# Two decode layers on one core: a new transfer and clock model in the kernel's own planner, and value loads of at most two quarters

## The chip, the cores and the metric

The kernel runs on one core of a Trainium2 chip. The metric is the device time of one execution in microseconds (us); lower is better. The engines are named as the profile names them: PE is TensorE (PEld its weight loads), DVE is VectorE, ACT is ScalarE, POOL is GpSimd and SP is SyncE, which here does nothing but issue DMAs.

## What is computed

Two identical layers follow each other for a batch of 8 sequences with one new token each. A layer is attention over a cache of 4096 positions (16 query heads on 8 cached heads, head size 256) and a small mixer with an MLP.

```python
def _A_ref(x, k_cache, v_cache, wq, wo):
    B, Sq, D = x.shape                      # 8, 1, 448
    Hq, Dh = 16, 256
    Hkv = k_cache.shape[1]                  # 8
    rep = Hq // Hkv
    q = (lambda x, *d: x.transpose(*d))((x @ wq).reshape(B, Sq, Hq, Dh), 0, 2, 1, 3)
    k = jnp.repeat(k_cache, rep, axis=1)    # cache: (8, 8, 4096, 256)
    v = jnp.repeat(v_cache, rep, axis=1)
    scores = jnp.einsum("bhqd,bhkd->bhqk", q, k) * (Dh ** -0.5)
    p = _softmax(scores, axis=-1)
    o = jnp.einsum("bhqk,bhkd->bhqd", p, v)
    return (lambda x, *d: x.transpose(*d))(o, 0, 2, 1, 3).reshape(B, Sq, Hq * Dh) @ wo
...
x = A_x
x = x + _A_ref(_layernorm(x, axis=-1), A_k_cache, A_v_cache, A_wq, A_wo)
x = x + _B_ref(_layernorm(x, axis=-1), B_w1, B_w2, B_w3, B_w4)
x = x + _A_ref(_layernorm(x, axis=-1), A_k_cache, A_v_cache, A_wq, A_wo)
x = x + _B_ref(_layernorm(x, axis=-1), B_w1, B_w2, B_w3, B_w4)
```

`_B_ref` shifts parts of its hidden vector along a sequence of length 1, which leaves zeros, so what is left of it is a layer norm and the MLP with `w3` and `w4`. Both layers read the same two caches of 134 MB each. All arrays are bfloat16.

## The kernel before, in words

**Tiles.** One cached head of one sequence, K or V, is 2 MB. It is split into four quarters ("units") of 512 KB: 128 partitions with 4 KB each. SBUF holds 30 slots of one quarter (`QUARTERS`). A DMA fetches up to four neighbouring quarters of one head at once into neighbouring slots: 512, 1024, 1536 or 2048 KB.

**What is kept.** Sequence by sequence the first layer runs over heads 0 to 7, and the second layer follows for the same sequence. Of the five "kept" heads 3 to 7, K stays in its slots from the first layer to the second (heads 3 to 6 wholly, head 7 in part), and of V seven quarters stay: all of head 7 and three of head 6 (`KEEP_K`, `KEEP_V`). Heads 0 to 2 are the "free heads": nothing of them is kept, and both layers load them. When the kept heads of a sequence are all in place, some 24 of the 30 slots are taken, and six go round.

**Work on one head.** `front()` transposes the fresh K quarters on PE (L1319, 128x128 blocks into PSUM, copied back by DVE L1250 or ACT L1251), makes the scores (L1043), and takes the softmax on DVE, POOL and ACT. `back()` multiplies with V (`pv`, L1149: eight 256-column matmuls for a quarter), adds up (`osum`, L1173), and multiplies with four rows of `wo` (`wor`, L1198). A K quarter that isn't kept gives its slot back after its score matmuls, a V quarter after its `pv`.

**Between the layers.** `mid()` runs a chain of small dependent steps for one sequence: the output of the attention is turned (L984, L987), the MLP's first product takes 56 matmuls (L838), gelu follows, its second product takes 70 (L984, L987), then come the second layer's queries (L822) and the scores on the kept K. Around this chain stand, as work that does not depend on it, the `back()` parts of the *next* sequence's three free heads, with 12 V quarters. They pass through the six slots that go round.

**The planner.** The order of the instructions is not that of the source. Every piece of work is an `Op` with an engine, a cost and dependencies. `Plan.schedule()` goes through them with a clock of its own, always takes the engine that is free first, and there the ready op with the best priority. The result is one fixed order for each engine, with semaphores. SP is in order: loads are issued in the order of their `prio`. For the next load, `next_kv()` picks how many quarters go into it (up to `most`), the slots, and so the PE instruction that it has to wait for. `late` (L203) is the time up to which it holds a load back for a longer run of free slots: `LEAD` before the planned end of the transfers in progress.

**Costs in the plan.** A load of n quarters takes `((n << 15) / 26.88e3 + 8 * 0.008) / FASTER` us (L628), that is 4.705 us for four. The transfers stand in one line with one end, `dma_end`. For PE, the planner counts "columns" in windows of 3.413 us (`WIN`). Below `COLS` of them it plans the next window with PE at the slow one of two costs. Where PE would wait and the columns of the last window are under `TARGET`, it puts in fillers: matmuls of 256 or 512 columns without use (L1522). A matmul of the chain counts `width` columns (20 to 24), a `pv` op 512, a `wor` op 448. PE's instructions are fetched in blocks of 128 pairs (`BLOCK`), at least 6 us apart (`FETCH`).

**MOST.** `back()` sets `most`, the largest load of V: `MOST` for free heads in the first layer (from the second sequence on), `MOST2` for one kept head in the second layer, 4 otherwise.

Of the kernel before, what the change touches and what calls it, by code (L numbers as in the profile page):

```python
# [32 lines left out]
BOOST = None  # L33
HOTK = 7
L2 = (3, 4, 2, 1, 0)
MOST = 4
MOST2 = 4
BACKS = (0, 1, 3)
MIX = "KKKKKFFF"
# [1 line left out]
PV0 = 0  # L41
PV1 = 0
QW, HW, YW = 24, 24, 12
SC = 448
YC = 0
Q1 = 176
# [30 lines left out]
class Plan:  # L77
# [5 lines left out]
    HOT = 3500  # L83


    ISSUE, LEAD = 4.0, 5.0
    BLOCK, FETCH = 128, 6.0
    LAT = {"pe": 0.25, "dve": 0.06, "act": 0.06, "pool": 0.05, "sp": 0.4}

    def __init__(self):  # L90
        self.ops = []
# [41 lines left out]
    def fetched(self, t, d, n, pairs, next_block):  # L133

        per = d / n
        while n:
            room = self.BLOCK - pairs % self.BLOCK
            if room == self.BLOCK:
                t = max(t, next_block)
                next_block = t + self.FETCH  # L140
            k = min(n, room)
            pairs += k
            n -= k
            t += k * per
        return t, pairs, next_block

    def schedule(self):
# [18 lines left out]
        for o in self.ops:  # L166
            if not left[o]:
                release(o, 0.0)
        dma_end = 0.0
        win, cols, warm = 0, 0, False  # L170
        recent, hot = [], False
        bank_ev = {}
# [5 lines left out]
        n = 0  # L178
# [14 lines left out]
        def next_kv(i):  # L193

            u = sp_next[i].unit
            m = 1
            while m < u.most and i + m < len(sp_next) and sp_next[i + m].unit is not None and \
                    sp_next[i + m].unit.tile is u.tile and sp_next[i + m].unit.u == u.u + m and \  # L200
                    sp_next[i + m].unit.keep == u.keep:
                m += 1
            late = max(free["sp"], dma_end - self.LEAD)  # L203
            times = sorted(set(x for x in self.free_at if x < 1e9))
            if not times:
                return None
            for t in [max(free["sp"], times[0])] + [x for x in times if free["sp"] < x <= late]:
                fit = [(k, a) for k, a in runs(t) if k >= m]
                if fit:
                    break  # L210
            else:
                t = max(late, times[0])
                m = min(m, max(k for k, a in runs(t)))
                fit = [(k, a) for k, a in runs(t) if k >= m]

            before = sp_next[i - 1].unit if i else None
            if before is not None and before.tile is u.tile:
                for k, a in fit:
                    if a <= before.slot + 1 <= a + k - m:
                        return t, m, before.slot + 1  # L220
            k = min(k for k, a in fit)
            fit = [a for k2, a in fit if k2 == k]
            q = min(fit) if u.keep else max(fit) + k - m
            return t, m, q

        while n < len(self.ops):
# [103 lines left out]
            order[e].append(o)  # L330
            n += 1
            if e == "sp":
                free[e] = t + 0.45
                start = max(t + self.ISSUE, dma_end)
                dma_end = start + o.dur
                end = dma_end
            else:
                d = o.dur
                if e == "pe":

                    w = int(t / self.WIN)
                    while win < w:
                        warm = cols >= self.COLS
                        cols = 0
                        win += 1
                    cols += d[2]
                    recent.append((t, d[2]))
                    end, pairs, next_block = self.fetched(t, d[0] if warm else d[1], d[3],
                                                          pairs, next_block)
                    d = end - t  # L350
                elif isinstance(d, dict):
                    d = d[e]
                end = free[e] = t + d
# [109 lines left out]
def bass_interleave_layers__gqa_block_cached__mixer_s_mlp__decode_kernel(  # L463
# [137 lines left out]
        return bass.AP(tensor=ap.tensor, offset=ap.offset, ap=[list(x) for x in ap.ap[:-1]] + [[0, P]])  # L601


    FASTER = 1.05

    def dma(name, dst, src, nbytes, sem, val, wr, at, row=8192):

        us = nbytes / 16 / 26.88e3 + nbytes / row / 16 * 0.008
        plan.op("sp", lambda eng: eng.dma_start(dst, src), us / FASTER, name, wr=wr, prio=at,
                dma=(sem, val))  # L610

    def dma_once(name, parts, keys, at, also=()):
# [7 lines left out]
    def issue_kv(o, n, q):  # L620

        (cache, b, h), u = o.unit.tile, o.unit.u
        src = cache[b, h].rearrange("(m s) d -> m (s d)", m=P)[:, u * 2048:(u + n) * 2048]
        dst = kv[:, q * 2048:(q + n) * 2048]
        slot_n[q] += 1
        o.emit = lambda eng: eng.dma_start(dst, src)
        o.dma = (slot_sem[q], 16 * slot_n[q])
        o.dur = ((n << 15) / 26.88e3 + 8 * 0.008) / FASTER  # L628

    plan.issue_kv = issue_kv  # L630

# [61 lines left out]
    def pe(fn, n, rd=(), wr=(), banks=(), name="chain", prio=None, width=20):  # L693

        if prio is None:
            prio = urge[0] + len(plan.ops)
        d = 0.06 + 0.026 * n
        return plan.op("pe", fn, (d, max(d, 0.06 + n * width / 1200), width * n, n), name, rd=rd, wr=wr, banks=banks, prio=prio)

    def mark(o):  # L700

# [424 lines left out]
    def back(layer, b, h):  # L1126
# [15 lines left out]
        for u in range(4):  # L1142

            def pv(t, u=u, q=vs[u]):
                last = None
                for s in range(8):
                    i = 8 * u + s
                    g4 = 32 * (i % 4)
                    last = t.matmul(ps[g4:g4 + 2, PV0:PV0 + DH], pT[nr][:, i, :],  # L1149
                                    slot_ap(q, s * 256, 256), start=(i < 4), stop=(i >= 28),  # L1150
                                    skip_group_check=True, tile_position=(0, g4))
                return last
            o = plan.op("pe", pv, (0.25, 0.46, 512, 8), "pv",
                    rd=[("pT", nr, 0), ("pT", nr, 1), ("s", vs[u], 0), ("s", vs[u], 1),
                        "pz"],
                    wr=[("pv", par, x) for x in range(u, 4)], banks=[bk])
            if u == 0:
                o.tbank = bk
            if u not in keep_v:
                o.frees = vs[u]  # L1160
# [31 lines left out]
        if k < HKV:  # L1192
            def wo_row(t):
                last = None
                for i in range(4):
                    a = (4 * h + i) * D
                    r = 64 * layer + 32 * (i % 2)
                    last = t.matmul(psR[r:r + 1, 0:D], oT[no][:, i % 2, i // 2:i // 2 + 1],  # L1198
                                    wo_sb[:, a:a + D], start=(k == 1 and i < 2),
                                    stop=(k == HKV - 1 and i >= 2),  # L1200
                                    skip_group_check=True, tile_position=(0, r))
                return last
            o = plan.op("pe", wo_row, (0.41, 0.78, 448, 4), "wor", rd=[("oT", no), "wo0"], wr=[kr],
                        banks=["R"], prio=hi)
            if k == HOTK and layer == 0:
                o.hot = True
# [375 lines left out]
```

## Time and profile before

| | us |
|---|---|
| median of 3 runs | 1109.96 |
| the three runs | 1104.91, 1109.96, 1110.28 |
| the profiled execution, its own time | 1105.82 |
| its span, first to last instruction | 1104.0 |
| mean granted clock of PE | 0.929 |

The span is what the profile's views divide up; 1.8 us of the profiled execution lie around it. "Idle before" in a group's line is the engine's idle time just before these instructions, with what ended it. "DMA share" is the mean busy share of the 16 DMA engines. A window's line gives, for a stretch of the span, each engine's busy time with the number of its instructions, then the granted clock of PE (1 is full), the DMA share and the rate in GB/s.

### The profile page before, as it was taken

To read this page: it belongs to the slowest core of one execution; us is meant where nothing else is said; L and a number is where in the kernel's file an instruction comes from. 1 tells how busy PE (TensorE), PEld (TensorE's weight loads), DVE (VectorE), ACT (ScalarE), POOL (GpSimd) and SP (SyncE) were. 2 spreads that over 40 slices of the span, in tenths; PEclk is the share of its full clock that TensorE was granted. 3 is DMA by queue.
4 is the path that set the end of the run, shared out by engine and by line. 5 is a ranking of instruction groups with operands and counts; after the bars stand their busy time and mean duration, and the time that the engine had idled before them with its cause. 6 is when DMAs were issued, how large, how long until landed. Compare 5 with 4: busy or idle time off the path is not lost.

```text
span 1104.0 us, 42700 instructions
## 1 busy us (share of the span) xinstructions
PE 964.3 (87%) x19509; PEld 772.5 (70%) x19509; DVE 577.7 (52%) x1829; ACT 294.5 (27%) x867; POOL 97.9 (9%) x275
## 2 busy tenths in 40 slices
PE   4888889898899888998889988899879998799997
PEld 4678557785578756787668865688557986597683
DVE  4245445654455544665446554555535755365554
ACT  1133112331124302343123411234123430243130
POOL 0000000000100101010010100001010010111010
PEclk9889899998999979999799998999989997999797
DMA  9999999999999999999999999999999999999993
GB/s 331 407 425 421 392 376 423 424 416 387 384 422 422 421 364 416 424 425 413 373 425 424 422 364 388 425 424 416 378 417 423 424 365 383 410 420 399 321 385 152
DMA packets 59871, 436.94 MB, mean 396 GB/s; under 512 B 6430, under 2 KB 9644, under 8 KB 36396
## 3 DMA queue, kind: packets, MB, share of 16 engines
q1 hardware_dynamic: 59684, 434.22, 97.0%
q8 instruction: 153, 2.51, 0.9%
q14 instruction: 26, 0.21, 0.0%
q10 hardware_dynamic: 8, 0.00, 0.0%
HBM read 434.18 MB, written 0.01 MB: 393 GB/s over the span
## 4 chain that ended last, share of the span: by engine, by line
PE 55%; DMA 35%; issue 4%; DVE 4%; ACT 1%; SPq 1%; POOL 0%; DVEq 0%
PE psT L1319 20%; DMA kv<-in_A_k_cache_dram 17%; PE psM L1043 14%; DMA kv<-in_A_v_cache_dram 14%; PE psP L1149 9%; DMA wo_sb<-in_A_wo_dram 4%; PE psR L1198 3%; PE psM L822 2%; PE psM L984 1%; DVE oS L1165 1%; PE psM L987 1%; DVE oS L1163 1%; PE psP L1173 1%; PE psP L1522 1%; PE psM L838 1%
## 5 line engine op out<-in xcount | busy, mean ns | idle before, releaser
L1319 PE MATMUL psT<-ident_f,kv 128*128 128x128 f32 x2752 | 381.2, 283 | 13.9 <-DMA kv<-in_A_k_cache_dram 13.8
L1250 DVE COPY kv<-psT 128x512 f32<-128x512 f32 x403 | 276.2, 690 | 155.4 <-PE psT L1319 151.7
L1319 PEld LDWEIGHTS psT<-ident_f,kv 128*128 128x128 f32 x2752 | 304.0, 144 | 38.2 <-issue 18.9
L1251 ACT COPY kv<-psT 128x512 f32<-128x512 f32 x317 | 184.8, 587 | 465.8 <-PE psT L1319 375.8
L1149 PE MATMUL psP<-kv,pT 128*2 128x256 bf16 x4096 | 185.6, 291 | 37.5 <-DMA kv<-in_A_v_cache_dram 20.1
L1043 PEld LDWEIGHTS psM<-q2T,kv 128*128 128x128 bf16 x3968 | 121.5, 99 | 50.0 <-issue 41.0
L1043 PE MATMUL psM<-q2T,kv 128*128 128x48 bf16 x3968 | 137.2, 186 | 19.9 <-issue 19.0
L1043 PEld LDWEIGHTS psM<-q1b,kv 128*128 128x128 bf16 x4032 | 131.6, 97 | 18.2 <-issue 8.6
L1043 PE MATMUL psM<-q1b,kv 128*128 128x48 bf16 x4032 | 140.4, 184 | 4.4 <-ACT pT L1116 2.6
L1149 PEld LDWEIGHTS psP<-kv,pT 128*2 128x2 bf16 x4096 | 80.6, 84 | 78.4 <-issue 30.7
L1106 POOL PARTITION_ALL_REDUCE gm<-pm x128 | 45.6, 356 | 761.0 <-DVE pm L1104 693.9
L1116 ACT ACTIVATE pT<-sS,nb,fac 128x32 bf16<-128x32 f32 x128 | 52.7, 417 | 145.4 <-DVE nb L1110 145.4
L1099 DVE COPY sS<-psM 128x64 f32<-128x64 f32 x128 | 28.6, 224 | 109.8 <-PE psM L1043 107.2
L1163 DVE CAST oS<-psP 128x256 bf16<-128x256 f32 x128 | 54.0, 422 | 57.6 <-PE psP L1149 55.8
L1198 PE MATMUL psR<-wo_sb,oT 128*1 128x448 bf16 x448 | 68.3, 390 | 5.5 <-DMA wo_sb<-in_A_wo_dram 3.2
L1120 POOL PARTITION_ALL_REDUCE Db<-rs x128 | 51.1, 400 | 209.3 <-ACT pT L1116 209.3
L1116 ACT ACTIVATE pT<-sS,nb 128x32 bf16<-128x32 f32 x128 | 40.9, 326 | 70.1 <-DVE nb L1110 70.1
L1173 PE MATMUL psP<-sel,oS 128*128 128x2 bf16 x512 | 32.1, 166 | 29.2 <-DVE oS L1165 26.7
L1173 PEld LDWEIGHTS psP<-sel,oS 128*128 128x128 bf16 x512 | 25.4, 100 | 45.1 <-DVE oS L1165 41.8
L1165 DVE TENSOR_TENSOR oS<-psP,oS 128x256 bf16<-128x256 f32 x128 | 54.2, 423 | 3.4
L822 PEld LDWEIGHTS psM<-x2c,wq_sb 128*128 128x128 bf16 x768 | 30.8, 98 | 17.1 <-issue 5.7
L1179 DVE TENSOR_TENSOR oT<-psP,rc 128x4 bf16<-128x4 f32 x128 | 20.2, 157 | 40.3 <-PE psP L1173 34.2
(172 smaller groups left out, 657.8 us busy)
## 6 DMA issues: line engine op xcount, KB each, us to landing
kv<-in_A_k_cache_dram SPq DMA_DIRECT2D x64, 2048.0 KB, 18.7
kv<-in_A_v_cache_dram SPq DMA_DIRECT2D x49, 2048.0 KB, 15.1
kv<-in_A_v_cache_dram SPq DMA_DIRECT2D x161, 512.0 KB, 7.9
kv<-in_A_v_cache_dram SPq DMA_DIRECT2D x36, 1024.0 KB, 10.2
kv<-in_A_k_cache_dram SPq DMA_DIRECT2D x44, 512.0 KB, 8.0
kv<-in_A_k_cache_dram SPq DMA_DIRECT2D x10, 1536.0 KB, 17.0
kv<-in_A_v_cache_dram SPq DMA_DIRECT2D x9, 1536.0 KB, 17.6
kv<-in_A_k_cache_dram SPq DMA_DIRECT2D x11, 1024.0 KB, 13.5
```

What stands on the lines that cost most here:

```text
L822: last = t.matmul(bank[:, at + i * step:at + i * step + copies], w, r, start=(kc == 0), stop=(kc == 3))
L1043: last = t.matmul(ps[:, SB + 2 * i:SB + 2 * i + 2 * REP], a()[:, c:256:2], bcast(rhs(c), REP, 1), start=(c == 0), stop=(c == 1))
L1116: return a.activation(pT[nr][:, :, :].rearrange("p i j -> p j i")[:, jj, :], sview[:, jj, :], ACT.Exp, bias=nb[nm][:, jj:jj + 1], scale=sc ...
L1120: plan.op("pool", lambda gp: gp.partition_all_reduce(Db[nr][:, :], rs[nr][:, :], P, RO.add), 0.5, "sum", rd=[("rs", nr, 0), ("rs", nr, 1)] ...
L1149: last = t.matmul(ps[g4:g4 + 2, PV0:PV0 + DH], pT[nr][:, i, :], slot_ap(q, s * 256, 256), start=(i < 4), stop=(i >= 28), skip_group_check= ...
L1163: plan.op("dve", lambda v: v.tensor_copy(oS[:, 0, :], po), 0.36, "o", rd=[("pv", par, x) for x in range(4)], wr=["oS0"], banks=[bk], prio=hi)
L1165: plan.op("dve", lambda v: v.tensor_tensor(oS[:, 1, :], po, oS[:, 0, :], ALU.subtract), 0.36, "o", rd=["oS0"] + [("pv", par, x) for x in r ...
L1173: last = t.matmul(ps[:, PV1 + 2 * c:PV1 + 2 * c + 2], oS[:, w, c:DH:2], sel[:, :], start=(w == 0), stop=(w == 1))
L1198: last = t.matmul(psR[r:r + 1, 0:D], oT[no][:, i % 2, i // 2:i // 2 + 1], wo_sb[:, a:a + D], start=(k == 1 and i < 2), stop=(k == HKV - 1 ...
L1250: return e.tensor_copy(dst, psT[bank][:, :])
L1251: return e.copy(dst, psT[bank][:, :])
L1319: last = t.transpose(psT[bank][:, s * P:(s + 1) * P], src, ident_f[:, :])
```

## The change

`Plan` gets 16 rings, one for each DMA engine, in place of one line of transfers: a load adds its cost to each ring, with `WAKE` more where the ring had run dry, and lands `LAND` after the last of them. A block of PE's instructions that is fetched adds `FETCH_DMA` to one ring, in turn one of the eight even ones. `ISSUE` goes from 4.0 to 1.0, `LEAD` from 5.0 to 4.0 and is measured from the mean of the rings, the latency of a DMA's signal from 0.4 to 0.05, SP's time for an issue from 0.45 to 0.4. `FASTER` goes, and a load of n quarters costs `(n << 15) / 27.2e3 + 8 * 0.009`, 4.891 us for four. In the count of columns, a matmul of the chain has 16 (`CW`) in place of its width, a `pv` op 568 in place of 512, a `wor` op 756 in place of 448. `MOST` goes from 4 to 2. `KEEP_V` stays at 7. No arithmetic on the tensors is changed.

```diff
-MOST = 4
+MOST = 2
 MOST2 = 4
...
+CW = 16
...
-    ISSUE, LEAD = 4.0, 5.0
+    ISSUE, LAND, LEAD = 1.0, 0.46, 4.0
+    RING, CARRY, WAKE = 16, (0, 2, 4, 6, 8, 10, 12, 14), 0.75
+    FETCH_DMA = 1.55
     BLOCK, FETCH = 128, 6.0
-    LAT = {"pe": 0.25, "dve": 0.06, "act": 0.06, "pool": 0.05, "sp": 0.4}
+    LAT = {"pe": 0.25, "dve": 0.06, "act": 0.06, "pool": 0.05, "sp": 0.05}
...
             if room == self.BLOCK:
                 t = max(t, next_block)
                 next_block = t + self.FETCH
+                c = self.CARRY[self.fetches % len(self.CARRY)]
+                self.fetches += 1
+                self.ring[c] = max(self.ring[c], t + self.ISSUE) + self.FETCH_DMA
...
-        dma_end = 0.0
+        self.ring, self.fetches = [0.0] * self.RING, 0
...
-            late = max(free["sp"], dma_end - self.LEAD)
+            late = max(free["sp"], sum(self.ring) / self.RING - self.LEAD)
...
             if e == "sp":
-                free[e] = t + 0.45
-                start = max(t + self.ISSUE, dma_end)
-                dma_end = start + o.dur
-                end = dma_end
+                free[e] = t + 0.4
+                for i in range(self.RING):
+                    wake = self.WAKE if t + self.ISSUE > self.ring[i] + 0.02 else 0.0
+                    self.ring[i] = max(t + self.ISSUE, self.ring[i]) + wake + o.dur
+                end = max(self.ring) + self.LAND
...
-    FASTER = 1.05
...
-        plan.op("sp", lambda eng: eng.dma_start(dst, src), us / FASTER, name, wr=wr, prio=at,
+        plan.op("sp", lambda eng: eng.dma_start(dst, src), us, name, wr=wr, prio=at,
                 dma=(sem, val))
...
-        o.dur = ((n << 15) / 26.88e3 + 8 * 0.008) / FASTER
+        o.dur = (n << 15) / 27.2e3 + 8 * 0.009
...
-        return plan.op("pe", fn, (d, max(d, 0.06 + n * width / 1200), width * n, n), name, rd=rd, wr=wr, banks=banks, prio=prio)
+        return plan.op("pe", fn, (d, max(d, 0.06 + n * width / 1200), CW * n, n), name, rd=rd, wr=wr, banks=banks, prio=prio)
...
-            o = plan.op("pe", pv, (0.25, 0.46, 512, 8), "pv",
+            o = plan.op("pe", pv, (0.25, 0.46, 568, 8), "pv",
...
-            o = plan.op("pe", wo_row, (0.41, 0.78, 448, 4), "wor", rd=[("oT", no), "wo0"], wr=[kr],
+            o = plan.op("pe", wo_row, (0.41, 0.78, 756, 4), "wor", rd=[("oT", no), "wo0"], wr=[kr],
```

Since the planner writes the order of all engines, these edits move instructions everywhere. The two built programs differ as follows:

| | before | after |
|---|---|---|
| PE matmuls | 19509 | 19624 |
| fillers of 256 columns (L1522) | 170 | 279 |
| fillers of 512 columns (L1522) | 61 | 67 |
| K and V loads of 512 / 1024 / 1536 / 2048 KB | 205 / 47 / 19 / 113 | 208 / 45 / 18 / 114 |
| quarters loaded in all | 808 | 808 |
| copies of transposed K on DVE / ACT | 411 / 317 | 427 / 301 |

## The prediction

> **What bounds the kernel now.** I read the page first: span, engines, and the rows of rate.
>
> ```profile
> span 1104.0 us, 42700 instructions
> PE 964.3 (87%) x19509; PEld 772.5 (70%) x19509; DVE 577.7 (52%) x1829; ACT 294.5 (27%) x867; POOL 97.9 (9%) x275
> ...
> DMA  9999999999999999999999999999999999999993
> GB/s 331 407 425 421 392 376 423 424 416 387 384 422 422 421 364 416 424 425 413 373 425 424 422 364 388 425 424 416 378 417 423 424 365 383 410 420 399 321 385 152
> DMA packets 59871, 436.94 MB, mean 396 GB/s; under 512 B 6430, under 2 KB 9644, under 8 KB 36396
> ```
>
> The transfers never rest and do at best about 425 GB/s. 436.94 MB at 424 GB/s are 1030.5 us, so 73.5 us of the span are lost: at both ends, and in dips that come once a sequence, some 130 us apart, in which the rate falls to 364 to 388. The change moves the same 808 quarters, so only these 73.5 us can move. Next, windows: one in mid-stream, then the dip at 530 us and the one at 655 (the eight dips are called by their times: 135, 268, 398, 530, 655, 790, 925, 1030).
>
> ```profile
> 600.00:620.00 20.00, 19.26 (x384) 18.19 (x380) 12.24 (x33) 7.99 (x23) 2.26 (x6) 1.00 1.00 423
> ...
> 520.00:530.00 10.00, 8.25 (x182) 6.09 (x182) 5.22 (x25) 0.00 (x0) 0.40 (x1) 0.83 0.96 382
> 530.00:540.00 10.00, 9.26 (x202) 6.08 (x196) 4.31 (x25) 0.21 (x1) 0.00 (x0) 0.66 0.97 353
> ...
> 650.00:660.00 10.00, 7.70 (x191) 5.75 (x193) 6.11 (x30) 0.00 (x0) 0.19 (x1) 1.00 0.76 302
> 660.00:670.00 10.00, 8.02 (x178) 5.30 (x178) 3.56 (x20) 0.21 (x1) 0.00 (x0) 0.65 0.89 317
> ```
>
> In the stream DMA sets the pace at 423 GB/s. In a dip six slots go round, the loads wait for `pv` to give them back, PE runs through the chain of `mid()`, and its clock (the third number from the end) falls to 0.65. The dip at 655 is deep: DMA share 0.76. Who waits for whom, first SP and then PE:
>
> ```profile
> SPq L626 <- PE psP L1149: 462.1, 141, 19.9
> SPq L626 <- PE psM L1043: 373.5, 90, 26.8
> ```
> ```profile
> PE psP L1149 <- DMA kv<-in_A_v_cache_dram: 20.1, 29, 2.0
> PE psT L1319 <- DMA kv<-in_A_k_cache_dram: 13.8, 14, 2.9
> ```
>
> SP waits nearly always, which costs nothing while loads are queued. PE's 20.1 us before `pv` (L1149) matter: asked by stretch they are 1.7, 3.7, 2.2, 1.3, 4.2, 2.3, 1.5 and 1.0 us in the eight dips, 17.9 together. There PE stands in front of a V quarter that hasn't landed, the chain stands behind it, and so do the slots.
>
> **The change part by part.** Sums are made against the profiled execution, 1105.82 us.
>
> *Bytes and sizes.* 808 quarters before and after, 384 K and V loads against 385, sizes nearly alike: 0 us.
>
> *Free heads' values in halves.* With `MOST` 4, a run of four slots was awaited for one such load in a dip: V of head 0 of the sixth sequence, at 646. Its slots wait for a `pv` of the sequence before, and its first `pv` for all of 2 MB.
>
> ```profile
> 652.45 1.04 PE L1149 MATMUL psP<-kv,pT 128*2 128x256 bf16 x32 [1.18 <-DMA kv<-in_A_v_cache_dram]
> ...
> 658.05 1.26 PE L1149 MATMUL psP<-kv,pT 128*2 128x256 bf16 x40
> 659.97 0.39 PE L1149 MATMUL psP<-kv,pT 128*2 128x256 bf16 x8 [0.66 <-DMA kv<-in_A_v_cache_dram]
> ```
>
> Between 653 and 658 no value matmul runs, no slot comes back, and DMA runs dry at 660. In the new order this head is two loads of 1024 KB, the first released by a score matmul some 8 us of PE work earlier, and two of its `pv` stand ahead of the chain. The price: the dip at 530 moved (382 + 353) x 10 us = 7.35 MB in 20 us, this one (302 + 317) x 10 us = 6.19 MB. The missing 1.16 MB at 424 GB/s are 2.7 us. Bounds 0 and -2.7, I take -2.7. In the dip at 135 a load of three becomes 2 + 1; 304 GB/s at 140 to 150 us against 353 is 0.49 MB, 1.2 us: bounds 0 and -1.2, I take -0.6.
>
> *Sizes, page against row.* The Trainium skill (DMA: Bandwidth & Descriptors, Measured) asks for batches of 1 MiB and more and shows 341 GB/s for one of 1 MB alone. By it two halves would take 12.3 us where one load in the stream takes 5, and the term would be a loss of 7 us. The windows differ: from 540 to 550, with nothing but 512 KB loads in a full queue, DMA moved 392 GB/s. I go by the windows.
>
> *The transfer model.* The old cost of 2 MB is 4.705 us, 446 GB/s, a rate that no slice of the page has; 2 MB at 424 GB/s take 4.95 us, and the new cost is 4.891. The old planner put `pv` where it believed V had landed, some 5% early on a long queue, and PE, in order, then stands there. Of the 17.9 us in the dips, 4.2 belong to the dip above; 13.7 are left. Bounds: none goes, or all; in the other direction, `pv` now behind the chain could hold slots longer (its price under the rivals). In the new order the `pv` between the last transpose and the chain's 56 matmuls go from 10, 11, 10, 8, 10, 13 and 13 to 10, 10, 11, 10, 10, 10 and 10 (dips 268 to 1030): no clear push either way. I take a third, -4.6 us, since another wait often ends just after the one that goes.
>
> *A load that grows.* Ahead of the dip at 925, V of head 7 was four loads and becomes one of 2048 KB. They landed at 912.7 to 916.6, so its first quarter can come 3.9 us later. Bounds 0 and +3.9, I take +1.5, since PE is busy with transposes until 913.7 there.
>
> *Fillers.* 109 more of 256 columns, 6 more of 512. Nine in a row take 1.19 us (649.95), so 0.114 us each; three of 512 take 0.84, 0.22 each: 12.4 + 1.3 = 13.7 us of PE. What hides them: PE's waits for data. In the stream PE is busy 17 to 19.3 of 20 us, and and most new ones stand there in clusters of two to eleven; ahead of the chain in the dips 268 to 790, 93 become 87. If the cover is gone they cost all 13.7, if it holds 0; I take +1.
>
> *Activity weights.* The clock's half-speed stretch in the dip at 925 is the longest.
>
> ```profile
> 922.30:936.00 13.70, 13.55 (x292) 9.45 (x289) 8.15 (x42) 0.22 (x1) 0.00 (x0) 0.50 0.99 369
> ```
>
> Here the fillers ahead of the chain go from 2 to 17. If half of these 13.7 us came back to full speed, 3.4 us would be won; if none, 15 x 0.114 = 1.7 are lost. I take -1, nearer the middle.
>
> *Weights, page against row.* The Trainium skill (TensorE: Matmul & The Clock Gate, What's actually happening) says that the activity window runs free of the kernel, that the transition point moves from run to run, and that one shouldn't fit to a count of cold matmuls. Weights fitted anew would then win nothing, and the sum would be 1.0 us higher. The windows show half speed in the same place, inside the chain, in dip after dip (0.66 at 530, 0.65 at 660, 0.50 here), which looks more like cause than chance; no run here shows the run-to-run part.
>
> *The sum:* -2.7 - 0.6 - 4.6 + 1.5 + 1.0 - 1.0 = -6.4, so 1099.4 for an execution like the profiled one. The median of the three runs lies 4.1 above that one: 1103.5. I say 1103, 0.6% below 1109.96.
>
> **The rivals.** (a) *Nothing that can be told.* Half a per cent, 5.5 us, is about what a measurement of this kernel can tell from no change. For it: 423 GB/s in the stream can't be bettered, the loads come in the same sequence, and a PE wait that ends in a dip may only uncover another, such as DVE's copy before L1173 (26.7 us in all). With the -4.6 at 0 and the halves at half, the sum is -0.4: 1109.5.
>
> (b) *Slower: fillers in PE's way.* Place: the startup, the clusters in the stream and the dip at 925. All 13.7 us on the path, with the halves' -2.7 kept: +11, 1121. It decides where a filler stands at a wait that in truth is over, PE falling behind by more than the queued loads, 15 us or so. Against it: PE's waits for K in the stream (13.8 us) are there to be filled. For it: PE is at 19.26 of 20 us in the window shown. From half of them uncovered (+6.9, with all gains gone) it is slower by over 0.5%.
>
> (c) *Faster by far.* All of the 17.9 us go and the clock holds in the dip at 925: 17.9 + 1.2 + 3.4 = 22.5, so 1087.5 against the median. Against it: DVE's copies of oS stand in the same places.
>
> (d) *Slower: values behind the chain.* If in each of seven dips the slots come back later by the chain's first 56 matmuls (1.55 us, 656.50 to 658.05), that is +10.9, 1120.8. Against it are the counts above; only the dips at 398, 925 and 1030 have fewer `pv` ahead.
>
> **How the numbers follow.** The forecast (1098 to 1104.4) gets 0.37, (a) 0.31, (b) 0.16, (c) 0.06, (d) 0.10. Faster by over 0.5% is the forecast and (c): 0.43. Same is (a): 0.31. Slower is (b) and (d): 0.26. Cases of both signs hold much, so the forecast's own range, 1098 to 1104.4, stands beside the wide one: down to 1089, short of (c)'s full price, and up to (b)'s 1121; some 2 in 10 are left outside, most of it above.
>
> **What would show it.** The 20 us of the dip at 655 should move 7 MB or more, with DMA share above 0.9 in each half. PE's wait for V before L1149 should fall from 20.1 to some 10 us. The stream should stay at 420 to 425 GB/s; if it falls, (b) is right, and PE would be busy 20 of 20 us there. The dip at 925 should show a shorter half-speed stretch than 13.7 us. I am wrong if waits for V fall and the dips' rate does not rise: then something else sets the pace in a dip. I am also wrong if a stretch that was in order before, such as 880 to 910, opens a new hole behind the larger load.

## The result, and the profile after

The changed kernel takes 1113.11 us in the median of 16 runs, the kernel before 1107.02 beside it: a ratio of 1.0061 with a 95% interval of 1.0040 to 1.0082. It is slower by some 6.7 us by the ratio (6.1 us between the medians), where 1103 and "faster" had the best chance. A second set of runs of the same kernel gave 1.0040 (1.0025 to 1.0056); both intervals lie above 1. Where a mean of the two is used below, it is 1.0050.

First the page of the changed kernel: span, engines, rate, and the first line of the chain that ended last.

```profile
span 1110.8 us, 42920 instructions
PE 973.8 (88%) x19624; PEld 780.4 (70%) x19624; DVE 591.1 (53%) x1848; ACT 285.2 (26%) x848; POOL 97.7 (9%) x275
...
GB/s 330 409 425 421 392 404 426 422 409 371 412 424 424 416 359 421 424 403 392 335 425 423 419 392 385 423 424 394 335 398 426 424 400 359 410 421 389 333 368 167
...
PE 72%; DMA 12%; DVE 8%; issue 5%; ACT 1%; SPq 1%; POOL 0%; DVEq 0%
```

The same line of the kernel before:

```profile
PE 55%; DMA 35%; issue 4%; DVE 4%; ACT 1%; SPq 1%; POOL 0%; DVEq 0%
```

Before, a third of the chain was transfers that PE waited for. Now it is an eighth: PE no longer stands in front of data, data stand in front of PE. PE's and SP's waits of the changed kernel say the same (engine and line, what it waited for, us in all, times, longest):

```profile
PE psP L1154 <- DMA kv<-in_A_v_cache_dram: 3.9, 8, 0.8
PE psT L1324 <- DMA kv<-in_A_k_cache_dram: 3.6, 3, 1.9
```
```profile
SPq L631 <- PE psM L1048: 532.9, 103, 26.6
SPq L631 <- PE psP L1154: 307.2, 137, 16.8
```

Of 33.9 us of waits for V and K, 7.5 are left. The windows of the changed kernel show what became of the dips (the engines stand in the order PE, PEld, DVE, ACT, POOL):

```profile
600.00:620.00 20.00, 19.26 (x368) 18.21 (x368) 13.26 (x33) 7.83 (x22) 2.26 (x6) 1.00 1.01 425
530.00:540.00 10.00, 9.52 (x212) 6.38 (x208) 4.79 (x27) 0.21 (x1) 0.00 (x0) 0.50 0.86 299
650.00:660.00 10.00, 7.47 (x156) 4.51 (x144) 4.87 (x18) 0.72 (x4) 0.75 (x2) 1.00 0.99 398
660.00:670.00 10.00, 9.07 (x203) 5.87 (x201) 4.29 (x24) 0.22 (x1) 0.00 (x0) 0.52 0.94 347
770.00:780.00 10.00, 9.33 (x193) 8.16 (x189) 5.96 (x17) 4.75 (x14) 1.51 (x4) 1.00 0.90 345
790.00:800.00 10.00, 8.14 (x219) 5.71 (x220) 5.25 (x28) 0.21 (x1) 0.00 (x0) 1.00 0.72 238
```

The dip at 655 is mended: (398 + 347) x 10 us = 7.45 MB where 6.19 were moved. The dip at 530 lost (353 before, 299 now, from 530 to 540), and at 790 there is a new hole. The kernel before, in those last two stretches:

```profile
770.00:780.00 10.00, 9.35 (x188) 7.30 (x186) 5.81 (x14) 3.02 (x9) 1.12 (x3) 1.00 1.02 414
790.00:800.00 10.00, 8.43 (x219) 5.66 (x216) 6.14 (x34) 0.21 (x1) 0.00 (x0) 0.80 0.99 348
```

(414 + 348 - 345 - 238) x 10 us = 1.79 MB, 4.2 us at 424 GB/s. The whole dip, from 770 to 810 us, says the same: 15.40 MB before, 13.45 after, 4.6 us less of transfers. At the last landing the changed kernel is 7.2 us behind: 1096.1 against 1088.9.

### The profile page after: what moved, and what is told of

It reads as the page before. It is cut to its first block, busy times and chain, and to the rows that moved or that the text cites. A ratio compares the mean times of both kernels' runs of the same rounds, so it can differ in the third digit from the quotient of the medians.

```text
span 1110.8 us, 42920 instructions
## 1 busy us (share of the span) xinstructions
PE 973.8 (88%) x19624; PEld 780.4 (70%) x19624; DVE 591.1 (53%) x1848; ACT 285.2 (26%) x848; POOL 97.7 (9%) x275
## 4 chain that ended last, share of the span: by engine, by line
PE 72%; DMA 12%; DVE 8%; issue 5%; ACT 1%; SPq 1%; POOL 0%; DVEq 0%
PE psT L1324 27%; PE psM L1048 18%; PE psP L1154 11%; DMA kv<-in_A_k_cache_dram 8%; PE psR L1203 4%; DMA kv<-in_A_v_cache_dram 3%; PE psP L1527 2%; PE psM L827 2%; DVE oS L1170 2%; DVE oS L1168 2%; PE psP L1178 2%; PE psM L989 2%; PE psM L992 1%; DMA w3x_sb<-in_B_w_dram 1%; DVE kv L1255 1%
## 5 line engine op out<-in xcount | busy, mean ns | idle before, releaser
L1324 PE MATMUL psT<-ident_f,kv 128*128 128x128 f32 x2752 | 375.5, 281 | 5.4 <-DMA kv<-in_A_k_cache_dram 3.6
L1255 DVE COPY kv<-psT 128x512 f32<-128x512 f32 x419 | 288.1, 690 | 150.4 <-PE psT L1324 145.0
L1256 ACT COPY kv<-psT 128x512 f32<-128x512 f32 x301 | 175.7, 587 | 465.8 <-PE psT L1324 378.0
L1154 PE MATMUL psP<-kv,pT 128*2 128x256 bf16 x4096 | 181.4, 292 | 19.8 <-issue 15.8
L1527 PE MATMUL psP<-ident_f 128*128 128x256 bf16 x279 | 49.5, 293 | 0.0
```

Source lines behind the costliest of these rows:

```text
L1255: return e.tensor_copy(dst, psT[bank][:, :])
L1256: return e.copy(dst, psT[bank][:, :])
L1324: last = t.transpose(psT[bank][:, s * P:(s + 1) * P], src, ident_f[:, :])
L1527: return t.matmul(dst, ident_b, bcast(ident_b[:, 0:n // 4], 4, 1), start=True, stop=True)
```

## The experiments

Five theories stand against each other. F: the slower planned transfer brings fillers, and those in the stream (the stretches between the dips) stand in PE's way, PE falls behind, slots come back late, the next dip deepens; this is rival (b). L: the new model holds loads back (LEAD 4, ISSUE 1), the queue is thin ahead of the dips. M: the halves cost. W: the new activity weights cost. O: any new order draws its dips anew. All ratios are to the kernel before, run on the same chip, with 95% intervals; 0.001 is 1.1 us.

**The three parts alone.** The halves, the weights, and the planner's transfer model, each put into the kernel before (of the weights and the model, the main lines):

```diff
-MOST = 4
+MOST = 2
```
```diff
-... width * n, n), name
+... CW * n, n), name
-(0.25, 0.46, 512, 8), "pv"
+(0.25, 0.46, 568, 8), "pv"
-(0.41, 0.78, 448, 4), "wor"
+(0.41, 0.78, 756, 4), "wor"
```
```diff
-    ISSUE, LEAD = 4.0, 5.0
+    ISSUE, LAND, LEAD = 1.0, 0.46, 4.0
+    RING, CARRY, WAKE = 16, (0, 2, 4, 6, 8, 10, 12, 14), 0.75
...
-        o.dur = ((n << 15) / 26.88e3 + 8 * 0.008) / FASTER
+        o.dur = (n << 15) / 27.2e3 + 8 * 0.009
```

The halves: 

> The kernel before with loads of at most 2 MB in halves alone (MOST 4 to 2), planner model and weights as before. Fillers 232 (before 231). Theory F (the slower planned transfer adds fillers that stand in PE's way) and theory L (loads held back by the new model) both put the loss elsewhere: ratio 0.996 to 1.000, the dip at 655 mended by about 2.7 us as the prediction had it. Rival M (the split itself costs, smaller loads run the queue dry in the dips at 530 and 790): 1.004 or more.

The weights: 

> The kernel before with the new activity weights alone (16 columns counted for each matmul of a helper, 568 and 756 for pv and wo). Fillers 223. F and L: within 0.3% of before (0.997 to 1.003), since fillers do not grow and the loads' order stays. Rival W (the weights move the clock's half-speed stretches to a worse place): 1.004 or more, with a lower granted clock in one of the dips.

The model: 

> The new transfer model alone (16 engines, fetches on eight, slower cost, LEAD 4, ISSUE 1), MOST 4 and the old weights. Fillers 350. F: carries the whole loss, 1.006 to 1.010, PE's wait for V before the value matmuls falls to about 4 us and PE's share of the chain that ended last rises to about 70%. L: carries most of it, 1.004 to 1.008, dips at 530 and 790 deeper than before. M or W: near 1.000.

**The parts in pairs,** that is the change without its model, without its weights (the three old counts come back with `width`), and without its halves.

```diff
-MOST = 4
+MOST = 2
...
+CW = 16
```
```diff
-CW = 16
```
```diff
-MOST = 2
+MOST = 4
```

> The change without its planner model: MOST 2 and the new activity weights. Fillers 227. If the three parts simply add (0.9959 for the halves, 1.0042 for the weights, 1.0013 for the model): 1.000. F: near 0.997 to 1.000, few fillers, no loss. W (the weights spoil the order whatever else is changed): 1.000 to 1.003, and the changed kernel's loss is this one's plus the model's. If the parts interact through the whole order (theory O: each new order draws its dips anew): anything from 0.996 to 1.006.

> The changed kernel with the old weights: halves and new model. Fillers 367, more than the changed kernel has; the leads ahead of the dips at 530 and 790 (loads released for units 352, 448, 456, 552) as long as in the kernel before. Adding the parts: 0.997. F: 1.006 or more, since it has the most fillers. W: 0.995 to 0.999. L: 1.000 to 1.003, since the leads are back.

> The changed kernel with MOST 4: new model and new weights, loads of up to four slots. Fillers 372. Adding the parts: 1.0055. F: 1.006 to 1.010. W: 1.004 to 1.007. If the halves are what gains, this is 0.4% slower than the changed kernel: 1.010.

And the fastest part once more:

> The kernel before with MOST 2, once more, since it was the fastest of several. 0.994 to 0.998 if the first ratio (0.9959) was no luck; 0.998 to 1.001 if some of it was.

| | fillers | old model | new model |
|---|---|---|---|
| nothing else | 231 / 350 | 1 | 1.0013 (0.9992 to 1.0033) |
| halves | 232 / 367 | 0.9959 (0.9940 to 0.9978), again 0.9982 (0.9963 to 1.0000) | 1.0056 (1.0025 to 1.0087) |
| weights | 223 / 372 | 1.0042 (1.0023 to 1.0061) | 1.0069 (1.0046 to 1.0093) |
| both | 227 / 346 | 0.9985 (0.9965 to 1.0005) | 1.0061, again 1.0040 |

In each row the right column is slower (in the first and the third by less than the intervals). With means of what was run twice the steps are +0.0013, +0.0086, +0.0027 and +0.0065, on average +0.0048 or 5.3 us: on average the model carries the loss, and clear of the noise it does so only in company with the halves. The halves alone win 2 to 4.5 us, so M falls as it was put; beside the model and the old weights, though, they lose (1.0013 to 1.0056). The weights lose 0.4% alone (W's figure), 0.56% beside the model, 0.15% beside the halves, and nothing beside both (1.0056 to 1.0050). The parts don't add, and each theory missed a run: the model alone is too good for F and L, the weights alone too bad for them, the changed kernel with the old weights too slow for W and L. It looks as if each order had an effect of its own, of up to some 0.4%; no run takes it apart, so theory O can't be left out, and a single ratio of 0.2% says little here.

**What in the model: the cost or the holding back?** The old kernel with the slower cost alone; the changed one with the faster cost; the changed one with loads planned earlier.

```diff
-    FASTER = 1.05
+    FASTER = 1.0
```
```diff
-        o.dur = (n << 15) / 27.2e3 + 8 * 0.009
+        o.dur = ((n << 15) / 27.2e3 + 8 * 0.009) / 1.05
```
```diff
-    ISSUE, LAND, LEAD = 1.0, 0.46, 4.0
+    ISSUE, LAND, LEAD = 1.0, 0.46, 8.0
```

> The kernel before with one number changed: FASTER 1.05 to 1.0, so 2 MB are planned at 4.94 us and not at 4.705. One transfer queue, ISSUE 4, LEAD 5, MOST 4 and the old weights stay. Fillers 342 (before 231). F (the slower cost brings fillers and is what loses): 1.004 to 1.007, PE's waits for K and V from 34 us to under 15. L (the new ring model and its short LEAD lose): 0.998 to 1.002. O (any new order draws its dips anew): 0.996 to 1.006.

> The changed kernel with its load cost divided by 1.05 again (2 MB at 4.66 us), everything else of the change kept: ring of 16, LEAD 4, ISSUE 1, MOST 2, new weights. Fillers 243, leads ahead of the dips at 530 as before (the one of units 552 stays at 20). F: 0.997 to 1.001, like the halves and weights without the model (0.9985). L: 1.004 to 1.007, since loads are held back as in the changed kernel.

> The changed kernel with LEAD 8 in place of 4: loads planned earlier, leads of units 352, 448 and 456 as before (26, 34, 20 us of PE work). Fillers 320. L: the loss goes, 0.998 to 1.002. F: 1.004 to 1.007, 26 fillers fewer being worth a tenth of a per cent at most.

Measured: 1.0023 (1.0003 to 1.0043), 1.0003 (0.9978 to 1.0027), 1.0085 (1.0053 to 1.0118). One number, the cost of a load made 5% smaller, takes the changed kernel's loss away with all else of the model in place, and the deep hole from 790 to 800 us with it (from 770 to 810 it moves 14.96 MB, where the changed kernel moves 13.45):

```profile
770.00:780.00 10.00, 9.24 (x176) 7.61 (x176) 5.73 (x15) 3.61 (x13) 1.15 (x3) 1.00 1.01 416
790.00:800.00 10.00, 7.78 (x193) 5.40 (x187) 4.14 (x24) 0.21 (x1) 0.00 (x0) 0.81 0.98 355
```

L falls: earlier planning gave back the longer leads and was slower still, and with the faster cost the short LEAD and ISSUE lose nothing. The slower cost alone loses too, but less than F expected, though it takes PE's waits for K and V down to 12.6 us, as F said.

**Fillers or order?** The cost changes both. So in the next runs the changed kernel's order of all useful work and of all loads stays, and only fillers are taken out of PE's list after the planning: the 133 in the stream; the other 213, near the turns of `mid()`, `wo` and the long chains; only the 75 in the stream between the dips at 268 and 790; only the 50 ahead of the dip at 268. In the run after those, the 75 are issued twice, and the last is the changed kernel once more. (`part` counts the chains of 56 matmuls ahead of a filler; each run has one of the four `keep` lines.)

```diff
+        def stays(f):
+            i = f.pos
+            return any(x.name in ("turn", "wo") or x.name == "chain" and x.dur[3] > 20
+                       for x in order["pe"][max(i - 14, 0):i + 22])
+        keep = [f for f in fills if stays(f)]                          # 133 out
+        keep = [f for f in fills if not stays(f)]                      # 213 out
+        keep = [f for f in fills if stays(f) or not 3 <= part(f) <= 6] # 75 out
+        keep = [f for f in fills if stays(f) or not 0 <= part(f) <= 2] # 50 out
+        order["pe"] = [o for o in order["pe"] if o.name != "warm" or o in keep]
```
```diff
+        for f in fills:
+            if not stays(f) and 3 <= part(f) <= 6:
+                f.emit = lambda t, once=f.emit: (once(t), once(t))[1]
```

> The changed kernel's own order of all useful work and of all loads, with 133 of its 346 fillers taken out of PE's list after the planning (213 left: those near turns, wo and the chain of 56 stay). F: the loss goes, 0.997 to 1.001 against before; score matmuls that release loads ahead of the dips at 530 and 790 come some 3 to 5 us earlier, and these dips recover 6 us each. L, M and W: the loss stays, 1.004 to 1.008, since the loads' order and the held-back issue are the same. A rival to F in the other direction: without fillers the clock falls in the stream and it is slower than the changed kernel (1.008 or more).

> The counterpart of the run with 213 fillers: the changed kernel's order with those 213 fillers taken out (the ones near turns, wo and the chain of 56) and the 133 in the stream left. If what counts is the number of fillers (each 0.114 us of PE): lower than the run with 213, about 0.998. If place counts (F in its narrow form: those in the stream stand in PE's way, those at the turns fill real waits and hold the clock): 1.006 or more, with more half-speed time at the turns.

> The changed kernel's order with only the 75 stream fillers between the dips at 268 and 790 taken out (271 left). F, with the place that the traces show (ground lost at the dips at 530 and 790): most of what the run with 213 fillers won comes back, 1.002 to 1.004, and the dip at 790 has no rate under 300 GB/s. If it is the fillers of the startup and of the first stretch: as the changed kernel, 1.005 to 1.007. If what the run with 213 won was chance: 1.005 to 1.007 too.

> The changed kernel's order with only the 50 stream fillers ahead of the dip at 268 taken out (296 left). F with place: as the changed kernel, 1.005 to 1.007, or worse, since the run with 213 was 1 to 2 us later up to 350 us. F by number alone: 0.15% won, 1.0045.

> The changed kernel's order with the same 75 stream fillers between the dips at 268 and 790 issued twice each, 75 matmuls more, some 8 us of PE at 0.114 us each. F: the loss grows by as much as the 75 cost, 1.008 to 1.013. If the fillers are covered and only the new order loses: as the changed kernel, 1.005 to 1.007.

> The changed kernel once more. All theories: 1.004 to 1.008. It shows how far one execution's trace can be read: if the dips at 530 and 790 lose 6 us each again against the trace of before, they are of the kernel; if other dips lose, the loss is spread and one trace shows only where it fell that time.

| the changed kernel's order, with | ratio | filler time in four stretches of the stream |
|---|---|---|
| 133 stream fillers out | 1.0020 (0.9994 to 1.0047) | |
| 75 of them out | 1.0019 (1.0004 to 1.0033) | 2.24 us |
| the other 50 out | 1.0020 (1.0005 to 1.0035) | |
| all in | 1.0061; 1.0040 | 13.21 us |
| 75 twice | 1.0088 (1.0067 to 1.0109) | 23.44 us |
| 213 at the turns out | 1.0123 (1.0095 to 1.0151) | |

The times of the last column are windows of the fillers' line alone. For the changed kernel (PE's busy time, then clock, DMA share and GB/s as before):

```profile
285.00:385.00 100.00, 2.66 (x16) 0.98 1.01 422
415.00:515.00 100.00, 2.15 (x13) 0.95 1.00 410
545.00:645.00 100.00, 3.25 (x18) 0.98 1.01 419
675.00:772.00 97.00, 5.16 (x25) 0.95 1.01 420
```

The kernel before has 0, 4, 1 and 4 there, 2.35 us. Each step of some 10 to 11 us of fillers costs 0.31% and 0.38%, 3.4 and 4.2 us, against the mean of the changed kernel's two ratios (0.21% and 0.48% against the second alone, which was run beside the others). Order and loads are the same in these three rows, so this part of the loss is the fillers', about 0.35 us for each us of them. From the 75 out to the 75 twice, 1.0019 to 1.0088, it is far clear of the noise; the lower step alone, 1.0040 to 1.0019, is so barely. The same matmuls at the turns earn: without those 213 the kernel is 0.7% slower, and the mean clock of the profiled execution falls from 0.942 to 0.891. So the place decides whether a filler costs or earns. What the 50 of the first stretch cost is less sure. Without them the ratio is 1.0020 against 1.0040, better than both of its forecasts, but within the intervals, and the traces don't decide it: behind them, at 390 us, its loads land 0.2 us later than in one execution of the changed kernel and 3.2 us earlier than in the other. All 133 out win no more than either group, so the small terms don't add.

How it works is seen between the dips at 655 and 790. PE's longest waits from 675 to 772 us, first before, then after (the second list is whole: PE waits for no DMA there):

```profile
PE psP L1149 <- issue: 3.7, 2, 2.0
PE psP L1173 <- DVE oS L1165: 2.5, 3, 1.0
PE psM L822 <- issue: 2.1, 2, 1.3
PE psT L1319 <- DMA kv<-in_A_k_cache_dram: 1.4, 2, 0.9
```
```profile
PE psM L1048 <- issue: 4.7, 3, 2.1
PE psP L1178 <- DVE oS L1170: 3.1, 3, 1.0
PE psM L1048 <- ACT kh L1264: 0.6, 1, 0.6
PE psR L1203 <- DVE oT L1184: 0.3, 1, 0.3
```

By the landings and starts in the trace, the K quarter that was used soonest in this stretch had been there for 1.7 us in the changed kernel; in the kernel before, and with the 75 fillers out, PE caught up with the transfers (0.0 us). The timeline of the changed kernel shows one cluster (start, length, instruction, how many):

```profile
762.51 0.58 PE L1203 MATMUL psR<-wo_sb,oT 128*1 128x448 bf16 x4 [0.25 <-DVE oT L1184]
763.02 1.89 PE L1527 MATMUL psP<-ident_f 128*128 128x256 bf16 x8
764.70 3.13 PE L1324 MATMUL psT<-ident_f,kv 128*128 128x128 f32 x20
```

By the plan's own clock the K quarter of these transposes lands at 745.47, 1.0 us after `wor` ends (744.45), so eight fillers go in between. On the chip `wor` ends at 763.1 and that quarter had landed at 761.42: nothing was left to wait for, and the cluster is 1.6 us of pure delay. (`wor` comes 18.6 us behind the plan and the quarter 16.0: PE has fallen 2.7 us further behind than the transfers, and this is what the plan doesn't see.) PE enters the dip late, the score matmul that gives slots back ahead of it comes late (its load is issued at 774.4, at 769.5 in the kernel before), and from 770 to 780 the DMA share is 0.90. That it is the kernel and not that one execution, the second profile of the changed kernel shows, and the one with the 75 fillers out:

```profile
530.00:540.00 10.00, 9.21 (x201) 5.28 (x200) 5.40 (x29) 0.21 (x1) 0.00 (x0) 0.75 0.95 347
770.00:780.00 10.00, 9.35 (x177) 8.04 (x173) 5.86 (x15) 4.33 (x15) 1.15 (x3) 1.00 0.94 360
790.00:800.00 10.00, 8.54 (x216) 6.34 (x216) 4.68 (x26) 0.21 (x1) 0.00 (x0) 0.89 0.71 243
```
```profile
770.00:780.00 10.00, 9.13 (x177) 7.68 (x175) 5.67 (x14) 3.97 (x14) 1.15 (x3) 1.00 1.01 413
790.00:800.00 10.00, 9.00 (x222) 6.39 (x218) 4.57 (x28) 0.21 (x1) 0.00 (x0) 0.74 0.94 326
```

All runs of this order make the same 405 transfers in the same sequence, so one and the same load can be followed through their traces. The table has the time from the landing of the K quarter behind the cluster to the issue of the load that waits for the score matmul; how long the queue still had work at that issue; and the time through the dip, from the landing of the K load ahead of it (776.28 in the changed kernel) to the landing of the eleventh load behind that one (803.50).

| fillers, of the changed kernel's | landing to issue, us | queue left, us | through the dip, us |
|---|---|---|---|
| all, two executions | 13.0, 13.1 | 3.1, 3.0 | 27.2, 27.0 |
| the 50 out | 13.1 | 3.7 | 26.1 |
| the 213 at the turns out | 12.3 | 4.0 | 26.8 |
| the 75 twice | 15.2 | 1.6 | 27.1 |
| the 75 out | 9.0 | 7.2 | 21.9 |
| the 133 out | 9.0 | 7.7 | 23.1 |

With the 75 in, the slot comes back some 4 us later and the dip lasts 4 to 5 us longer, in five executions against two: the hole at 790 belongs to the order with its fillers. Doubled, they delay the slot by 2 us more, but the dip is no longer than with them once, so what they cost on top falls elsewhere. The loss at 530 does not belong to them: 299 GB/s in one execution of the changed kernel, 347 in the other.

**Two tries at a better kernel.** The halves with 48 stream fillers out, and the halves with a still faster planned transfer.

```diff
-MOST = 4
+MOST = 2
...
+        keep = [f for f in fills if stays(f)]
```
```diff
-MOST = 4
+MOST = 2
...
-    FASTER = 1.05
+    FASTER = 1.10
```

> The kernel before with MOST 2, and 48 of its 232 fillers taken out of the stream after the planning (184 left). If fillers in the stream cost as in the pair changed kernel and the same with 133 fillers fewer (1.0061 against 1.0020, 0.031% for ten): 0.9959 - 0.0015 = 0.994, faster than both kernels. If a filler in the stream only costs where data are already there (F in its narrow form; before has PE waits for K and V of 34 us): no difference, 0.995 to 0.997.

> MOST 2 with the planned transfer made faster still, FASTER 1.10: 2 MB at 4.49 us. Fillers 184. If the cost's way goes on (1.0: +0.2%, 1.05: 0): 0.993 to 0.996, better than MOST 2 alone. If 1.05 is where PE's waits for data and its fillers balance: 0.997 to 1.003, with PE's waits for K and V above the 34 us of MOST 2.

Both missed: 0.9995 (0.9976 to 1.0014) and 1.0062 (1.0038 to 1.0086). With 1.10 the planner has 184 fillers, PE's waits for K and V (L1319, L1149) are 43.9 us (34.0 with the halves alone), and the mean clock is 0.907 against 0.930. So the halves with 1.10 lose against the halves with 1.05, and few fillers are no aim in themselves. Why 48 fewer did the halves no good is open. The halves alone, 0.9959 and 0.9982, are the only version that came out ahead of the kernel before in two tries; the two intervals overlap, so part of the first may have been luck.

## Why the prediction was wrong

*Halves, -2.7 and -0.6.* The first held, and by its own mechanism. From 650 to 670 us the kernel before moves 302 and 317 GB/s, the halves alone 369 and 354, again 377 and 381, the changed kernel 398 and 347, again 392 and 355. (1.26 MB at 424 GB/s are 3.0 us.) "7 MB or more, with DMA share above 0.9 in each half" came true. The halves alone win 4.5 and 2.0 us. But it is the size of this one load that decides there, and not `MOST`. With `MOST` left at 4, the weights alone, the model alone and the slower cost alone happen to fetch that head in two loads of 1024 KB as well, and move 7.26, 7.30 and 7.66 MB from 650 to 670 us; the changed kernel with `MOST` 4 fetches it at once, as the kernel before does, and moves 5.99 (before: 6.19). The model alone, then the changed kernel with `MOST` 4:

```profile
650.00:660.00 10.00, 8.41 (x160) 5.58 (x158) 5.53 (x16) 1.54 (x6) 0.75 (x2) 1.00 1.00 410
660.00:670.00 10.00, 7.65 (x206) 5.66 (x199) 4.98 (x26) 0.21 (x1) 0.00 (x0) 0.89 0.90 320
```
```profile
650.00:660.00 10.00, 8.00 (x152) 4.89 (x151) 5.23 (x22) 0.72 (x4) 0.76 (x2) 0.96 0.82 336
660.00:670.00 10.00, 7.71 (x196) 5.37 (x196) 5.12 (x27) 0.21 (x1) 0.00 (x0) 0.67 0.75 263
```

The first three, at 1.0042, 1.0013 and 1.0023, also show that this dip mended makes no faster kernel by itself. For the second term nothing is shown: from 140 to 150 us the rate rose from 304 to 377 and 370 GB/s in the changed kernel, but to 309 and 341 with the halves alone. Going by the windows, and not by the 341 GB/s of the Trainium skill's page (DMA: Bandwidth & Descriptors, Measured; its loads were issued from GpSimd), was right: two loads of 1 MB lost nothing in a full queue.

*Transfer model, -4.6.* This step failed. Its mechanism came true beyond what was asked: the wait for V fell from 20.1 to 3.9 us, not to "some 10". Its gain did not come. The model alone is the plainest test: PE's wait for V falls to 6.4 us, and the ratio is 1.0013 (0.9992 to 1.0033), where 4.6 us had been put down as won; on average over four pairs the model costs 5.3 us. PE's waits of the model alone:

```profile
PE psT L1323 <- DMA kv<-in_A_k_cache_dram: 6.5, 4, 2.7
PE psP L1153 <- DMA kv<-in_A_v_cache_dram: 6.4, 9, 1.1
```

"I am wrong if waits for V fall and the dips' rate does not rise" describes most of what happened. In windows of 30 to 40 us around the dips, before against the two executions after, the rate rose at 135 (368 GB/s to 389 and 389) and at 655 (356 to 376 and 387), fell at 790 (386 to 340 and 347), 925 (385 to 365 and 360) and 1030 (350 to 329 and 340), and went no clear way at 268, 398 and 530 (358 to 367 and 356, 366 to 364 and 359, 376 to 344 and 375). That PE's own work set the pace in place of the waits is argued from the chain over the whole span (PE 55% to 72%), not shown dip by dip. The likely reason, argued too: a PE that waits for the queue now and then has caught up with the transfers, so taking those waits away with later orders and fillers gained nothing, as DMA still had to fetch the same bytes.

*Fillers, +1.* This is the term that was mis-sized, and it comes of the step above: the fillers were hidden by "PE's waits for data", the very waits that the model was to take away. One wait was counted twice, as gain and as cover. The price of 13.7 us of PE was right as a bound; the runs put 2.3 to 3.4 us of loss on the 75 between the dips at 268 and 790, and no more, 2.2 to 3.3 us, on all 133 of the stream (the lower figures against the second measurement of the changed kernel, the higher against the mean of both). Rival (b) with half of them uncovered, +6.9, comes near the 6.7 us measured, and 0.16 was given for it. That its figure fits is luck: it is made of fillers alone, and the runs give them half of the loss or a little more. Its point of decision stands as it was put in its first half, "a filler stands at a wait that in truth is over"; "falling behind by more than the queued loads, 15 us or so" was too strict: between the dips at 655 and 790 the fillers took 5.16 us, and the slots ahead of the dip were 4 us late, with 3 us of loads left in the queue. The sign that was named for (b), a slower stream, hardly showed: in the four stretches it ran at 421, 421, 422 and 420 GB/s before, at 422, 410, 419 and 420 after, and at 420, 420, 418 and 417 in the second execution. The fillers' price fell due in the dip behind them.

*Larger load ahead of the dip at 925, +1.5.* From 910 to 940 the rate fell: 404, 391 and 343 GB/s before, 392, 362 and 313 after, again 342, 372 and 335. That is 0.71 and 0.89 MB, 1.7 and 2.1 us, as large as the term. But the changed kernel comes to this dip some us later, and over 880 to 960 us the rates are 384 before, 388 after and 373 in the second execution, so a loss is shown in one execution only. That the load is the cause wasn't tried.

*Weights, -1.* The clock did what the term asked, and the time did not follow. In the dip at 925 it rose from 0.62 and 0.70 to 1.00 and 0.68 in the halves of 920 to 940, and in the second execution to 1.00 and 1.00: by these figures 6.4 and 0 us of 13.6 at half speed are left. The dip got no faster for it. The weights lost 0.3% on average over their four pairs, from +0.56% to -0.06%. The rule that was weighed and set aside (the Trainium skill, TensorE: Matmul & The Clock Gate, What's actually happening: the transition point moves from run to run, don't fit to it) agrees with the traces: the same kernel had 0.68 and 1.00 from 930 to 940, and 0.50 and 0.75 from 530 to 540, in executions that lie up to some 3 us apart there. By it the term would have been 0.

*Rivals (a), (c), (d).* (c) is out. (d) wasn't needed: the hole at 790 goes with the fillers while the order of `pv` stays. For (a), the sum with the -4.6 at 0 and the halves at half is -0.15 and not -0.4; it makes no difference to what was expected.

*What stays open:* some 0.2% of the changed kernel's loss with fillers out (1.0020, 1.0019), why the model loses clearly only beside the halves, why the weights lose alone and not in company, and why fillers won't add up. Orders differ by a few tenths of a per cent for reasons that no run here names.

## What to carry to other kernels

A wait can be a gain to be had or a cover for other work, never both in one sum; when an edit removes waits, cost everything that was hidden in them at full price. A planner that fills a wait acts on its own clock: if data land later in it, measured against the engine that waits, than they do on the chip, its filling is real work in front of data that are there. So a cost a little too fast can beat the true one, and one faster still can lose again: here 1.0003 with the cost 5% smaller against 1.0061 and 1.0040 without, and 1.0062 with 1.10 in the kernel with the halves. Three values in two kernels show no more than that. To tell an order from its fillers, keep the order and take out or double the fillers, part by part.

## What the runs showed of the hardware

One kind of useless matmul is worth both signs: 213 at the turns hold PE's clock (0.942 with them, 0.891 without, 0.7% of time), 75 in the stream cost 0.2 to 0.4%. The hole at 790 is not made by PE's clock. In steps of 2 us, its deepest stretch moves 90 GB/s in one execution and 68 in the other, both at a clock of 1.00, while PE runs the chain's 56 matmuls; the half-speed stretch comes only behind it. The first execution, then the second:

```profile
794.00:796.00 2.00, 2.00 (x68) 1.58 (x57) 1.28 (x9) 0.00 (x0) 0.00 (x0) 1.00 0.43 90
802.00:810.00 8.00, 7.62 (x144) 4.62 (x141) 3.63 (x18) 0.00 (x0) 0.00 (x0) 0.50 1.00 367
```
```profile
792.00:794.00 2.00, 2.00 (x67) 1.67 (x60) 1.37 (x9) 0.00 (x0) 0.00 (x0) 1.00 0.34 68
```

And two executions of one kernel differ by 48 GB/s in one dip (299 and 347; followed load by load, the second gains 5.2 us from 506 to 550 us) and by 5 in another (238 and 243), so a dip is to be read from two traces before it is explained.
